# One written plan for five rounds of a mixed DFT and attention loop: the products with v in six blocks instead of ten, and the six score banks dealt in turn

## The chip, the cores and the metric

The kernel runs on one core of a Trainium2 chip. The metric is device time in microseconds (us): 1810.5 us is the median of three runs of the kernel before (1808.91 to 1810.7).

A core has engines that run their own queues of instructions in order: TensorE (PE in the profile, with its weight loads on a row of their own, PEld), VectorE (DVE), ScalarE (ACT), GpSimd (POOL) and SyncE (SP), which here issues nearly all transfers. PE writes its results into PSUM, which this kernel uses as eight banks of 128 x 512 float32; DVE and ACT read them from there.

## The reference, cut to what matters

```python
a = x @ dft_hid_re.T ; b = x @ dft_hid_im.T          # x: 2048 x 640
y = dft_seq_re @ a - dft_seq_im @ b                  # 2048 x 2048 matrices
q = (x @ wq) as 32 heads of 20 ; k = x @ wk ; v = x @ wv     # one k and v for all heads
p = softmax(q @ k.T * 20 ** -0.5)                    # per head 2048 x 2048
o = (p @ v) over heads @ wo
g = sigmoid((x * gate_w).sum(-1))
out = g * y + (1 - g) * o
```

Everything is float32. The kernel keeps that accuracy by splitting an operand into a high and a low part and adding three products.

## The kernel before, in words

**Before the main loop.** The first 250 us compute q, k, v and the gate, and then `a` and `b` of the hidden DFT (line 125), which go to DRAM and come back later as operands x. The first scores of the attention are computed there already.

**The main loop** mixes three streams of matmuls on PE, from about 249 us to 1623 us of the span.

- *Scores.* The heads come in 16 pairs p. Head 0 of a pair lies in rows 0 to 63 of the array, head 1 in rows 64 to 127, so a score matmul uses one half of the array's rows. Each score is computed twice. In the first pass (`a_unit`, line 330) 128 queries against 512 keys go to a PSUM bank, and DVE takes their maximum (line 337). In the second pass (`b_unit`, line 750) 128 keys against 512 queries go to a bank, with the maximum already subtracted through two more rows of the operand `qs`, and ACT takes the exponential into one of 16 SBUF buffers `pt` (line 759). A bank can be written again when its reader has ended.
- *Sequence DFT* (`y`, line 645). It is done as seven products of half-size blocks, 56 groups in all. In the main loop a group is one output block of 128 x 320. Its sum of 96 matmuls is halved over the two halves of the array's rows, 48 for each (16 steps j of three matmuls). [...] `Halves.run` makes the first y of a half after a turn wait for a score's reader that comes after the other half's last y (`mark`). The operands of a group come in two parts of eight steps, which POOL splits into high and low parts (`split_c`, lines 450 to 455) in one of three rotating buffers `ch`, `cl`. The 25th y of a half is the first that needs the second part.
- *Products with v* (`av_step`, line 763), "V" for short. One V takes four `pt` tiles (one step kc of 128 keys for both heads and two blocks of queries) and uses all 128 rows of the array in four groups of 32 columns. It adds into the bank "V".

A matmul on one half of the rows runs beside one on the other half. PE issues in order, so the written order decides what runs beside what.

**The order** is written out by hand. A round has eight a, eight b, 18 or 20 y and two V. `ROUND_10` is used three times and `ROUND_9` twice in five rounds. In a word like `a1S2` the digit is the half of the rows and the rest is the bank: the six banks S0 to S5 are written out by name for every score. `c` is a `b` that takes the newest free `pt` buffer. `E0` empties F0 with ACT (line 671) once in five rounds, after which POOL adds the block to earlier ones where the product needs that (lines 693 and 698). Each round is: seven scores of half 1 and nearly all y of half 0, one b across, V, then the mirror image, V. Each V handles a step whose scores came in the round before. One group y takes five rounds, and there are 48 times five rounds before the last pair of heads, which has its own round (`ROUND_LAST`, 16 times, with the two V side by side).

**The chain between pairs.** The a of a pair run 12 units (of 64 per half) ahead of the b. When the last a of a pair has been read, `tick()` (called at every second a) counts on; three ticks later `a_final` is issued: DVE transposes the maxima (`mt`, line 351), POOL splits them (`ms`, lines 352 and 353), SP writes them to DRAM (`m_d`) and reads them back into rows 60, 61, 124 and 125 of `qs` (four transfers `qs<-m_d`). The first b of that pair needs them.

Of the kernel before, what the change touches and what calls it, by code (L numbers as in the profile page):

```python
# [18 lines left out]
S = 2048  # L19
# [4 lines left out]
NT = S // P  # L24
NPAIR = H // 2
LAST = NPAIR - 1
HALF = D // 2
SJ = NT // 2
# [6 lines left out]
def kernel(  # L35
# [18 lines left out]
    psum = ctx.enter_context(tc.tile_pool(name="psum", bufs=1, space=PSUM))  # L54


    BANKS = {"A": ["S2", "S3", "S4"], "B": ["S0", "S1"], "F": ["S5", "F0"]}
    turn = {k: 0 for k in BANKS}

    def bank(tag, name):  # L60
# [308 lines left out]
    def tick():  # L369
        clock["n"] += 1  # L370
        due = [t for t in todo if t[0] <= clock["n"]]
        todo[:] = [t for t in todo if t[0] > clock["n"]]
        for _, f, args in due:
            f(*args)
# [4 lines left out]
    def a_half(hh, tag="A", main=False):  # L379
        u = state[hh]  # L380
        if u >= NA:
            return
        ins = a_unit(u, hh, tag)
        if main:
            halves.scored(ins)
        state[hh] = u + 1
        if state[1 - hh] <= u:
            return
        if u % 64 == 16 and u // 64 + 1 < NPAIR:
            load_qs(u // 64 + 1)  # L390
        if u % 64 == 63:
            later(1, a_reduce, u // 64)
            later(3, a_final, u // 64)
# [233 lines left out]
    class Halves:  # L627
# [3 lines left out]
            self.todo = [[], []]  # L631
            self.last = self.mark = None

        def put(self, ps2, w, x, start, stop):

            one = len(ps2) == 1
            for g, r in enumerate(RG):
                s0, s1 = start and not (one and g == 1), stop and not (one and g == 0)
                self.todo[g].append((ps2, w[r], x[r], s0, s1))

        def run(self, g):
            while not self.todo[g]:
                next(ys)
            ps, w, x, start, stop = self.todo[g].pop(0)
            mm = nc.tensor.matmul(ps[g % len(ps)], w, x, start=start, stop=stop)  # L645
            if len(ps) == 1:

                if not start and self.last != g:
                    tc.add_manual_dep(mm.ins, self.mark.ins.name, ORDER, reason="turns with a bank")
                self.last, self.mark = g, None  # L650
# [6 lines left out]
    halves = Halves()  # L657
# [3 lines left out]
    def y_evict():  # L661

        if not ended:
            return
        grp = ended[0]
        ps = grp["ps"]
        if "t" not in grp:
            grp["t"] = [op.tile([P, HALF], F32, name=("yt", "yu")[k]) for k in range(len(ps))]
            grp["left"] = list(range(len(ps)))
        k = grp["left"].pop(0)  # L670
        nc.scalar.activation(grp["t"][k], ps[k], AF.Copy)  # L671
        if not grp["left"]:
            ended.pop(0)
            y_out(grp)
# [4 lines left out]
    def y_in(n, k):  # L679

        got = []
        for q, (_, old, _) in enumerate(PRODUCTS[n][2]):
            if old is not None:
                t = op.tile([P, HALF], F32, tag=f"ya{q}", name="ya")
                move(t, y_block(old, k))
                got.append(t)
        return got
# [15 lines left out]
    def f_stream():  # L703

        load_c(0, 1)
        split_c(0, 1)  # L710
        for g, (n, k) in enumerate(GROUPS):
            ps = [bank("F0", f"y_{n}_{k}")[:, :HALF]]
            if g >= GMAIN:
                ps.append(bank("S5", f"y_{n}_{k}_1")[:, :HALF])
            y0 = y_in(n, k)
            for sh in range(2):
                h, l = c_ops.pop((g, sh))
                load_c(g + 1, sh)
                for j in range(SJ):
                    if j == SJ // 2:  # L720
                        split_c(g + 1, sh)
                        if sh == 0:
                            load_x(n + 1, k)
                        else:
                            split_x(n + 1, k)
                    jj = sh * SJ + j
                    x = x_ops[n, jj // 2]
                    hi, lo = x[:, jj % 2], x[:, 2 + jj % 2]
                    last = jj == NT - 1
                    halves.put(ps, h[:, j], hi, jj == 0, False)  # L730
                    halves.put(ps, h[:, j], lo, False, False)
                    halves.put(ps, l[:, j], hi, False, last)
                    if last:
                        ended.append({"n": n, "k": k, "ps": ps, "y": y0})
                    yield

# [7 lines left out]

    ptfree = list(range(16))

    def b_unit(p, hh, kc, qc, tag, newest):
        b = 64 * hh
        ps = bank(tag, f"b_{p}_{kc}_{qc}_{hh}")
        nc.tensor.matmul(  # L750
            ps,
            ks[b : b + 62, kc * P : (kc + 1) * P],
            qs[p][b : b + 62, qc * ROW : (qc + 1) * ROW],
            start=True,
            stop=True,
        )
        slot = ptfree.pop(-1 if newest else 0)
        t = pp.tile([P, ROW], F32, tag=f"pt{slot}", name="pt")
        halves.scored(nc.scalar.activation(t, ps, AF.Exp, scale=SCALE))  # L759
        pt[(hh, kc, qc)] = t, slot  # L760
# [4 lines left out]
    def av_step(p, qh, kc):  # L765
        if kc == 0:
            av[qh] = bank("V", f"av_{p}_{qh}")
        for hh in range(2):
            for j in range(2):
                t, slot = pt.pop((hh, kc, 2 * qh + j))  # L770
                av_mm(av[qh], 2 * hh + j, t, kc, kc == 0, kc == NT - 1)
                ptfree.append(slot)

    def finish_half(p, qh):
        ob = op.tile([P, ROW], F32, name="ob")
        nc.scalar.activation(ob, av[qh], AF.Copy)
        for hh in range(2):
            h = 2 * p + hh
            for j in range(2):
                js = slice((2 * qh + j) * ROW, (2 * qh + j + 1) * ROW)  # L780
                g = 32 * (2 * hh + j)
                move(sum_d[h : h + 1, js], ob[g + DH : g + DH + 1])
                move(oT_d[h * DH : (h + 1) * DH, js], ob[g : g + DH])
        if p == LAST:
            sm = op.tile([P, 16], F32, name="sm")
            ts = slice(qh * S // 2, (qh + 1) * S // 2)
            for hh in range(2):
                move(sm[64 * hh : 64 * hh + 64], sum_d[2 * p + hh, ts].rearrange("(s t) -> s t", t=16))
            later(4, finish_last, ts, sm)
        elif qh == 1:  # L790
            sm = op.tile([P, 32], F32, name="sm")
            move(sm, sum_d[2 * p : 2 * p + 2].rearrange("h (s t) -> (h s) t", t=32))
            later(24, finish_sums, p, sm)
# [11 lines left out]
    def finish_last(ts, sm):  # L805
# [10 lines left out]

    ROUND_10 = (
        "a1S0 y0 b1S3 y0 y0 c1S1 y0 y0 a1S2 y0 a1S5 y0 y0 a1S4 y0 b1S0 c0S3 V a0S1 y1 y1 b0S0 "  # L820
        "y1 y1 a0S5 y1 a0S3 y1 y1 b0S2 y1 y1 a0S4 y1 c0S0 c1S1 V y0"
    ).split()
    ROUND_9 = (
        "a1S2 y0 b1S0 y0 y0 a1S1 y0 a1S5 y0 y0 a1S4 y0 y0 b1S3 y0 c0S2 c1S0 V a0S5 y1 b0S2 y1 "
        "y1 a0S1 y1 c0S0 y1 y1 a0S3 y1 y1 a0S4 y1 E0 b1S2 c0S5 V"
    ).split()

    ROUND_LAST = (
# [3 lines left out]
    ).split()  # L832
    ROUNDS = [(p, qh, kk) for p in range(NPAIR) for qh in range(2) for kk in range(NT // 2)]

    BEFORE = {
        4: (lambda: load_wo(range(3)), lambda: load_o(0), lambda: load_o(1)),
# [1 line left out]
        6: (lambda: split_o(0), lambda: load_o(2)),  # L838
        7: (lambda: [load_y(tb) for tb in range(4)],),
    }  # L840
    old = []
    for rnd in ROUNDS:
        p, qh, kk = rnd
        nb, na = [0, 0], 0
        turn = (p * NT + qh * SJ + kk) % 5
        new = [(p, qh, 2 * kk), (p, qh, 2 * kk + 1)]
        for what in ROUND_LAST if p == LAST else ROUND_10 if turn < 3 else ROUND_9:
            if what == "V":
                if old:
                    st = old.pop(0)  # L850
                    av_step(*st)
                    if st[2] == NT - 1:
                        finish_half(*st[:2])
                continue
            g = int(what[1])
            if what[0] == "y":
                halves.run(g)
            elif what[0] == "E":
                if p == LAST or turn == 4:
                    y_evict()  # L860
            elif what[0] in "bc":
                b_unit(p, g, 2 * kk + nb[g] // 2, 2 * qh + nb[g] % 2, what[2:], what[0] == "c")
                if p == LAST and sum(nb) % 2 == 0:
                    tick()
                nb[g] += 1
            else:
                if na % 2 == 0:
                    tick()
                a_half(g, what[2:], True)
                na += 1  # L870
        old += new
        if p == LAST and qh == 1:
            for f in BEFORE.get(kk, ()):
                f()
    for _ in range(2):
        y_evict()
    split_o(1)
# [69 lines left out]
```

## Time and profile before

| What | Value |
|---|---|
| median of three runs | 1810.5 us |
| profiled execution: its span | 1807.7 us |
| rest, median less span | 2.8 us |
| PE busy | 1799.4 us (100%) |
| DVE busy | 1457.3 us (81%) |
| ACT busy | 1243.2 us (69%) |
| POOL busy | 822.1 us (45%) |
| granted PE clock, mean | 1.000 |

The columns of a group are: line, engine, operation, what it writes and reads, count, then busy time in us and mean ns of one, then idle time of the engine before them and what ended it. In a timeline the columns are start in us, length in us, engine, line, operation and count; neighbours of the same kind are merged into one row, "x8" says how many. One V shows as "x8", because each of its four matmuls stands twice in the records. Lengths of matmuls include their way through the array, so they overlap; the distance between starts is what one costs.

### The profile page before, as it was taken

Reading aid. Unit: us, or ns where it says so; the run is one execution under the profiler, and the core shown is the slowest. Engines: PE = TensorE matmul, PEld = TensorE weight load, DVE = VectorE, ACT = ScalarE, POOL = GpSimd, SP = SyncE. Lnnn points to the kernel's source line nnn. Section 1 sums busy time; section 2 is a strip of 40 time slices with the busy share of each in tenths; the row PEclk is TensorE's granted clock in tenths of the full one; section 3 lists DMA queues with packets and bytes.
Section 4 is the critical chain, followed back from the end, with each engine's and each line's share of the span. In section 5 each row is a group of like instructions: output and inputs, shape, how many; then the busy total and the mean of one; then the engine's idle time right before and its main releaser. Section 6 shows DMA issues by size and latency. Waiting matters only on the chain.

```text
span 1807.7 us, 40911 instructions
## 1 busy us (share of the span) xinstructions
PE 1799.4 (100%) x16342; PEld 1215.1 (67%) x16342; DVE 1457.3 (81%) x2335; ACT 1243.2 (69%) x2327; POOL 822.1 (45%) x559
## 2 busy tenths in 40 slices
PE   9999999999999999999999999999999999999999
PEld 7799976666666666666666666666666666657789
DVE  4469988888888888888888888888888888853354
ACT  5432247777777777777777777777777777776731
POOL 1012136444546464666655565565554444342241
PEclk9999999999999999999999999999999999999999
DMA  8763334332344433444353434353433342315666
GB/s 267 227 192 99 115 100 139 116 108 84 130 125 133 121 119 106 153 126 152 112 167 101 156 112 141 113 153 115 136 112 114 87 126 79 97 59 169 207 215 209
DMA packets 131003, 243.89 MB, mean 135 GB/s; under 512 B 26356, under 2 KB 77556, under 8 KB 128292
## 3 DMA queue, kind: packets, MB, share of 16 engines
q1 hardware_dynamic: 130012, 238.00, 41.8%
q0 software_dynamic: 800, 3.28, 0.6%
q8 instruction: 128, 2.10, 0.5%
q14 instruction: 63, 0.52, 0.1%
HBM read 194.62 MB, written 50.86 MB: 136 GB/s over the span
## 4 chain that ended last, share of the span: by engine, by line
PE 99%; DMA 0%; POOL 0%; ACT 0%; DVE 0%; issue 0%; SPq 0%; ACTq 0%
PE av L763 28%; PE y L645 20%; PE a L330 18%; PE b L750 15%; PE ab L125 8%; PE q L114 1%; PE o L114 1%; PE q L115 1%; PE q L116 1%; PE o L116 1%; PE o L115 1%; PE kv L210 0%; PE kv L211 0%; DMA xr<-in_xT_dram 0%; DMA xr<-x_d 0%; ACT pt L759 0%
## 5 line engine op out<-in xcount | busy, mean ns | idle before, releaser
L337 DVE TENSOR_REDUCE mx<-a 128x1 f32<-128x512 f32 x2048 | 1291.3, 684 | 170.0 <-PE a L330 164.6
L759 ACT ACTIVATE pt<-b 128x512 f32<-128x512 f32 x2048 | 1110.7, 597 | 334.9 <-PE b L750 289.9
L645 PE MATMUL y<-x,ch 64*128 64x320 f32 x3584 | 796.6, 317 | 1.1 <-ACT pt L759 1.1
L330 PE MATMUL a<-ks,qs 60*128 60x512 f32 x2048 | 740.0, 416 | 0.0
L645 PEld LDWEIGHTS y<-x,ch 64*128 64x128 f32 x3584 | 552.3, 184 | 85.5 <-ACT pt L759 83.5
L750 PE MATMUL b<-qs,ks 62*128 62x512 f32 x2048 | 596.5, 405 | 0.6 <-DVE mx L337 0.6
L330 PEld LDWEIGHTS a<-ks,qs 60*128 60x128 f32 x2048 | 379.8, 185 | 277.0 <-ACT pt L759 197.4
L763 PE MATMUL av<-pt,vsb 128*32 128x512 f32 x4096 | 542.0, 604 | 0.0
L645 PE MATMUL y<-x,cl 64*128 64x320 f32 x1792 | 528.3, 311 | 0.5 <-POOL cl L455 0.5
L645 PEld LDWEIGHTS y<-x,cl 64*128 64x128 f32 x1792 | 314.7, 184 | 42.0 <-ACT pt L759 41.1
L750 PEld LDWEIGHTS b<-qs,ks 62*128 62x128 f32 x2048 | 314.0, 185 | 23.4 <-issue 6.7
L450 POOL TENSOR_TENSOR craw<-craw 128x1024 f32<-128x1024 f32 x80 | 191.1, 2388 | 236.2 <-DMA craw<-in_cre_dram 88.8
L455 POOL TENSOR_TENSOR cl<-craw,ch 128x1024 fp32r<-128x1024 f32 x98 | 234.2, 2389 | 7.9
L454 POOL CAST ch<-craw 128x1024 fp32r<-128x1024 f32 x98 | 101.7, 1038 | 182.2 <-PE y L645 153.4
L763 PEld LDWEIGHTS av<-pt,vsb 128*32 128x32 f32 x4096 | 82.3, 108 | 139.8 <-issue 131.5
L125 PE MATMUL ab<-wh,xh 64*128 64x320 f32 x640 | 136.0, 307 | 0.0
L125 PE MATMUL ab<-wl,xh 64*128 64x320 f32 x640 | 135.8, 306 | 0.0
L125 PE MATMUL ab<-wh,xl 64*128 64x320 f32 x640 | 135.6, 305 | 0.0
L698 POOL TENSOR_TENSOR ya<-yt,ya 128x320 f32<-128x320 f32 x64 | 59.4, 944 | 142.8 <-ACT yt L671 142.2
L524 ACT ACTIVATE half<-ab 128x320 f32<-128x320 f32 x64 | 28.0, 438 | 114.1 <-PE ab L125 100.8
L125 PEld LDWEIGHTS ab<-wh,xl 64*128 64x128 f32 x640 | 98.7, 184 | 0.0
L125 PEld LDWEIGHTS ab<-wl,xh 64*128 64x128 f32 x640 | 98.6, 185 | 0.0
(88 smaller groups left out, 1082.7 us busy)
## 6 DMA issues: line engine op xcount, KB each, us to landing
craw<-in_cre_dram SPq DMA_DIRECT2D x96, 512.0 KB
craw<-in_cim_dram SPq DMA_DIRECT2D x96, 512.0 KB
xr<-x_d SPq DMA_DIRECT2D x88, 320.0 KB
qs<-qh_d SPq DMA_DIRECT2D x64, 160.0 KB
x_d<-both SPq DMA_DIRECT2D x64, 160.0 KB
ya<-y_d SPq DMA_DIRECT2D x64, 160.0 KB
y_d<-ya SPq DMA_DIRECT2D x64, 160.0 KB
xr<-in_xT_dram SPq DMA_DIRECT2D x20, 256.0 KB
```

Source lines behind the costliest of these rows:

```text
L114: nc.tensor.matmul(ps, wh, xh, start=(i == 0), stop=False)
L125: nc.tensor.matmul(ps, w[r], x[r], start=(i == 0 and k == 0), stop=(i == n - 1 and k == 2))
L330: nc.tensor.matmul(ps, qs[p][b : b + 60, qb * P : (qb + 1) * P], ks[b : b + 60, c * ROW : (c + 1) * ROW], start=True, stop=True,)
L337: return nc.vector.tensor_reduce(mx[p][:, hh, qb, c : c + 1], ps, axis=AX.X, op=ALU.max)
L450: eng.tensor_tensor(raw, raw, raws[1], op=PRODUCTS[n][0][1])
L454: eng.tensor_copy(h, raw)
L455: eng.tensor_tensor(l, raw, h.bitcast(F32), op=ALU.subtract)
L645: mm = nc.tensor.matmul(ps[g % len(ps)], w, x, start=start, stop=stop)
L698: nc.gpsimd.tensor_tensor(ya, yt, ya, op=how)
L750: nc.tensor.matmul(ps, ks[b : b + 62, kc * P : (kc + 1) * P], qs[p][b : b + 62, qc * ROW : (qc + 1) * ROW], start=True, stop=True,)
L759: halves.scored(nc.scalar.activation(t, ps, AF.Exp, scale=SCALE))
L763: nc.tensor.matmul(ps[32 * g : 32 * g + 32, :], vsb[:, kc, :], t, start=first, stop=last)
```

## The change

The rounds of five are replaced by one string `PLAN`, one letter for each instruction, which runs 48 times. Lower case is half 0 of the rows, capitals half 1: a/A and b/B are scores, y/Y the DFT, V a product with v, E the emptying of F0.

- The counts in a plan are those of five rounds before: 40 a, 40 b, 48 y and 48 Y, ten V and one E.
- The ten V stand in six blocks: two alone and four pairs. Between them lie stretches of 7, 46, 6, 18, 65 and 35 matmuls (the first reaches over the seam of two plans).
- The y of a plan are no longer mixed in ten turns of nine or ten: first 27 Y, then 9 y and 39 y, then 21 Y.
- The scores take the banks S0 to S5 in turn, whatever their reader, instead of by name.
- Every b takes the newest free `pt` buffer.
- A V handles the step that is two V behind (`LAG`); the scores are counted for each half by itself.
- `start` and `stop` of a group are decided when a matmul is issued, since either half may come first.
- `ROUND_LAST` and what follows are the same, written with the new counters.

```diff
-    BANKS = {"A": ["S2", "S3", "S4"], "B": ["S0", "S1"], "F": ["S5", "F0"]}
+    BANKS = {"S": ["S0", "S1", "S2", "S3", "S4", "S5"], "A": ["S2", "S3", "S4"], "B": ["S0", "S1"], "F": ["S5", "F0"]}
...
-            ps, w, x, start, stop = self.todo[g].pop(0)
+            ps, w, x, grp = self.todo[g].pop(0)
+            one = len(ps) == 1
+            k = 0 if one else g
+            start, stop = grp[k] == 0, grp[k] == (6 if one else 3) * NT - 1
+            grp[k] += 1
...
-        slot = ptfree.pop(-1 if newest else 0)
+        slot = ptfree.pop(-1)
...
-    ROUND_10 = (
-        "a1S0 y0 b1S3 y0 y0 c1S1 y0 y0 a1S2 y0 a1S5 y0 y0 a1S4 y0 b1S0 c0S3 V a0S1 y1 y1 b0S0 "
-        "y1 y1 a0S5 y1 a0S3 y1 y1 b0S2 y1 y1 a0S4 y1 c0S0 c1S1 V y0"
-    ).split()
-    ROUND_9 = (
-        "a1S2 y0 b1S0 y0 y0 a1S1 y0 a1S5 y0 y0 a1S4 y0 y0 b1S3 y0 c0S2 c1S0 V a0S5 y1 b0S2 y1 "
-        "y1 a0S1 y1 c0S0 y1 y1 a0S3 y1 y1 a0S4 y1 E0 b1S2 c0S5 V"
-    ).split()
+    PLAN = (
+        "BVaBYaYYbYYbYYaYbYYaYYbYaYYbYbYYaYbYYYaYbYYYaYaBVAbAaBbVVBayByyyAyByAyaAyByV"
+        "VAbyByAyyByyAyyByyAyByyAyyByyAyByByyyAyByAyyByByyAyAyyyAyByAyybAVVAbYYaYbY"
+        "YbYaYYbYaYYYaYYbYaYYbYaYYbYVVaBbAaE"
+    )
...
+    LAG = 2
+    taken = {"b": [0, 0], "a": 0, "V": 0}
+
+    def next_b(g, tag):
+        r, nb = divmod(taken["b"][g], 4)
+        p, qh, kc = STEPS[2 * r + nb // 2]
+        b_unit(p, g, kc, 2 * qh + nb % 2, tag)
+        taken["b"][g] += 1
+
+    def next_v():
+        st = taken["V"] - LAG
+        taken["V"] += 1
+        if st >= 0:
+            av_step(*STEPS[st])
+            if STEPS[st][2] == NT - 1:
+                finish_half(*STEPS[st][:2])
+
+    for what in PLAN * (LAST * NT // 5):
+        g = int(what in "ABY")
+        if what == "V":
+            next_v()
+        elif what == "E":
+            y_evict()
+        elif what in "yY":
+            halves.run(g)
+        elif what in "bB":
+            next_b(g, "S")
+        else:
+            if taken["a"] % 2 == 0:
+                tick()
+            a_half(g, "S", True)
+            taken["a"] += 1
```

More of the change, by code (lines that the diff above doesn't have):

```diff
@@ L632, in __init__, with put @@
             self.last = self.mark = None
-        def put(self, ps2, w, x, start, stop):
-            one = len(ps2) == 1
+        def put(self, ps2, w, x, grp):
             for g, r in enumerate(RG):
-                s0, s1 = start and not (one and g == 1), stop and not (one and g == 0)
-                self.todo[g].append((ps2, w[r], x[r], s0, s1))
+                self.todo[g].append((ps2, w[r], x[r], grp))
         def run(self, g):
@@ L643, in run @@
                 next(ys)
-            ps, w, x, start, stop = self.todo[g].pop(0)
+            ps, w, x, grp = self.todo[g].pop(0)
[3 more added lines that the diff above has]
+            grp[k] += 1
             mm = nc.tensor.matmul(ps[g % len(ps)], w, x, start=start, stop=stop)
-            if len(ps) == 1:
+            if one:
                 if not start and self.last != g:
@@ L715, in f_stream @@
             y0 = y_in(n, k)
+            grp = [0, 0]
             for sh in range(2):
@@ L728, in f_stream @@
                     hi, lo = x[:, jj % 2], x[:, 2 + jj % 2]
[L729 to L733, printed above, removed]
+                    halves.put(ps, h[:, j], hi, grp)
+                    halves.put(ps, h[:, j], lo, grp)
+                    halves.put(ps, l[:, j], hi, grp)
+                    if jj == NT - 1:
                         ended.append({"n": n, "k": k, "ps": ps, "y": y0})
@@ L745, with b_unit @@
     ptfree = list(range(16))
-    def b_unit(p, hh, kc, qc, tag, newest):
+    def b_unit(p, hh, kc, qc, tag):
         b = 64 * hh
@@ L812, in finish_last @@
             move(rx_d[h * DH : (h + 1) * DH, ts], rec_d[h : h + 1, ts].to_broadcast([DH, S // 2]))
-    ROUND_10 = (
-        "a1S0 y0 b1S3 y0 y0 c1S1 y0 y0 a1S2 y0 a1S5 y0 y0 a1S4 y0 b1S0 c0S3 V a0S1 y1 y1 b0S0 "
-        "y1 y1 a0S5 y1 a0S3 y1 y1 b0S2 y1 y1 a0S4 y1 c0S0 c1S1 V y0"
-    ).split()
-    ROUND_9 = (
-        "a1S2 y0 b1S0 y0 y0 a1S1 y0 a1S5 y0 y0 a1S4 y0 y0 b1S3 y0 c0S2 c1S0 V a0S5 y1 b0S2 y1 "
-        "y1 a0S1 y1 c0S0 y1 y1 a0S3 y1 y1 a0S4 y1 E0 b1S2 c0S5 V"
-    ).split()
+    PLAN = (
+        "BVaBYaYYbYYbYYaYbYYaYYbYaYYbYbYYaYbYYYaYbYYYaYaBVAbAaBbVVBayByyyAyByAyaAyByV"
+        "VAbyByAyyByyAyyByyAyByyAyyByyAyByyByyyAyByyAyyByByyAyAyyyAyByAyybAVVAbYYaYbY"
+        "YbYaYYbYaYYYaYYbYaYYbYaYYbYVVaBbAaE"
+    )
     ROUND_LAST = (
@@ L832 @@
     ).split()
-    ROUNDS = [(p, qh, kk) for p in range(NPAIR) for qh in range(2) for kk in range(NT // 2)]
+    STEPS = [(p, qh, kc) for p in range(NPAIR) for qh in range(2) for kc in range(NT)]
     BEFORE = {
@@ L840 @@
     }
[L841 to L847, printed above, removed]
-            if what == "V":
[L849 to L857, printed above, removed]
-            elif what[0] == "E":
[L859 to L863, printed above, removed]
-                    tick()
[L865 to L874, printed above, removed]
@@ L875 @@
+    for kk in range(NT):
+        for what in ROUND_LAST:
+            if what == "V":
+                next_v()
+            elif what[0] == "E":
+                y_evict()
+            elif what[0] == "y":
+                halves.run(int(what[1]))
+            else:
+                if sum(taken["b"]) % 2 == 0:
+                    tick()
+                next_b(int(what[1]), what[2:])
+        for f in BEFORE.get(kk - NT // 2, ()):
+            f()
+    old = STEPS[-LAG:]
     for _ in range(2):
```

## The prediction

> **What bounds the kernel now.** I read the page first, then the main loop alone (262 to 1620 us) as one stretch with PE's own list of waits, then the chain and PE's timeline.
>
> ```profile
> span 1807.7 us, 40911 instructions
> PE 1799.4 (100%) x16342; PEld 1215.1 (67%) x16342; DVE 1457.3 (81%) x2335; ACT 1243.2 (69%) x2327; POOL 822.1 (45%) x559
> L337 DVE TENSOR_REDUCE mx<-a 128x1 f32<-128x512 f32 x2048 | 1291.3, 684 | 170.0 <-PE a L330 164.6
> L759 ACT ACTIVATE pt<-b 128x512 f32<-128x512 f32 x2048 | 1110.7, 597 | 334.9 <-PE b L750 289.9
> ```
> ```profile
> 262.00:1620.00 1358.00, 1358.00 (x12107) 826.60 (x12107) 1187.97 (x1922) 1056.21 (x1970) 729.36 (x482) 1.00 0.39 120
> ```
> ```profile
> PE y L645 <- POOL cl L455: 0.5, 1, 0.5
> ```
>
> PE never stands still between 262 and 1620 us at full clock (1.00), and its one wait there is 0.5 us. DVE and ACT do stand still, and they wait for PE. So PE's written order is the time, and five rounds take, by two rows of the chain 36 cycles apart, (1312.48 - 279.89)/36 = 28.68 us:
>
> ```profile
> 279.89 1.01 PE av L763 x8
> ...
> 1312.48 1.02 PE av L763 x8
> ```
>
> **What one thing costs on PE.** A stretch between two V, from PE's timeline, and a pair of V from the last rounds:
>
> ```profile
> 1158.67 0.50 PE L330 MATMUL a<-ks,qs 60*128 60x512 f32 x1
> 1158.67 0.56 PE L645 MATMUL y<-x,ch 64*128 64x320 f32 x2
> 1159.01 0.40 PE L750 MATMUL b<-qs,ks 62*128 62x512 f32 x1
> 1159.07 0.31 PE L645 MATMUL y<-x,cl 64*128 64x320 f32 x1
> ...
> 1159.95 0.39 PE L330 MATMUL a<-ks,qs 60*128 60x512 f32 x1
> 1159.95 0.31 PE L645 MATMUL y<-x,cl 64*128 64x320 f32 x1
> ...
> 1160.52 1.06 PE L763 MATMUL av<-pt,vsb 128*32 128x512 f32 x8
> 1161.52 0.49 PE L330 MATMUL a<-ks,qs 60*128 60x512 f32 x1
> ```
> ```profile
> 1650.32 1.92 PE L763 MATMUL av<-pt,vsb 128*32 128x512 f32 x16
> 1652.17 0.73 PE L750 MATMUL b<-qs,ks 62*128 62x512 f32 x3
> ```
>
> Between 1159.0 and 1159.95 lie four scores (0.235 us each) and six y (0.147 each), side by side. The first score of a stretch takes 1159.01 - 1158.67 = 0.34, so a start costs 0.105. V to next start is 1.00 alone (0.995 before rounding) and 1652.17 - 1650.32 = 1.855 for two: 0.135 less than two alone. A stretch's floor is its fuller half: in six of the ten, 10 y and a score = 1.70; in four, seven scores = 1.64; together 16.8. With ten V, 16.8 + 9.95 = 26.75; the missing 1.93 are starts and ends, 0.195 for each stretch.
>
> **The change, part by part.**
>
> *PE's order.* The fuller half of the new stretches: 7 matmuls 3 scores = 0.70; 46: 27 Y and 2 B = 4.43; 6: 0.70; 18: 9 y and 2 a = 1.79; 65: 39 y and 2 b = 6.19; 35: 21 Y and A = 3.31. Sum 17.13, which is 0.36 more, since y pile up on one half. V: 2 x 0.995 + 4 x 1.855 = 9.41, 0.54 less. Starts and ends: 6 x 0.195 = 1.17, 0.78 less. Sum 27.71, so -0.96 us a cycle. All of it is on the path, as PE is.
>
> *Six banks in turn.* Now the n-th score waits for the reader of the (n-6)th, and a stretch holds up to 13 a. The readers' pace, and the delay from a score's start to its reader's:
>
> ```profile
> 602.28 0.20 DVE L351 STREAM_TRANSPOSE mt<-mxr 128x32 f32<-128x32 f32 x1
> 602.65 2.48 DVE L337 TENSOR_REDUCE mx<-a 128x1 f32<-128x512 f32 x4 [0.17 <-PE a L330]
> ```
> ```profile
> 602.12 0.50 PE L330 MATMUL a<-ks,qs 60*128 60x512 f32 x1
> ```
> ```profile
> 612.50 1.57 ACT L759 ACTIVATE pt<-b 128x512 f32<-128x512 f32 x3 [0.35 <-PE y L645]
> ```
>
> DVE: (2.48 - 0.68)/3 = 0.60 each, 0.53 after the score's start. ACT: (1.57 - 0.60)/2 = 0.49. Over a cycle that is 40 x 0.60 = 24.0 and 40 x 0.49 = 19.6, both under 27.7. Inside the stretches it is tight. In the 46, the last B needs the bank of the sixth a: 0.53 + 5 x 0.60 + 0.68 = 4.2, plus 0.05 for the release (below) 4.3; PE is there at 0.105 + 0.235 + 27 x 0.147 = 4.3. In the 65, the last A needs the ninth A: 0.53 + 8 x 0.60 + 0.68 + 0.05 = 6.1; PE is there at 6.1. In the 35 it is 3.1 against 3.2. The pairs of V need an exponential whose score stands last or last but one ahead of them: 0.53 + 0.60 after that score, while PE has a first V of 0.88 in between. So no stretch has a margin over 0.1. Bounds: 0 (all fits), and 0.13 for each of six stretches, 0.8. I take 0.25, near the low end, because every sum above comes out within 0.1 of PE. Cycle: -0.71.
>
> *The first cycle.* The second part of the first group is split late:
>
> ```profile
> 255.87 2.37 POOL L450 TENSOR_TENSOR craw<-craw 128x1024 f32<-128x1024 f32 x1 [10.82 <-DMA xr<-x_d]
> 258.30 1.04 POOL L454 CAST ch<-craw 128x1024 fp32r<-128x1024 f32 x1
> 259.42 2.37 POOL L455 TENSOR_TENSOR cl<-craw,ch 128x1024 fp32r<-128x1024 f32 x1
> ```
> ```profile
> 249.30 0.49 PE L750 MATMUL b<-qs,ks 62*128 62x512 f32 x1 [0.62 <-DVE mx L337]
> ...
> 261.84 0.41 PE L645 MATMUL y<-x,cl 64*128 64x320 f32 x1 [0.52 <-POOL cl L455]
> ...
> 278.00 0.49 PE L330 MATMUL a<-ks,qs 60*128 60x512 f32 x1
> ```
>
> Before, the 27th y of a half met this at its place in round 3 and waited 0.52 (cl ends at 261.79, so the release takes 0.05). Now 27 Y stand at the front: Y27 is reached at 249.3 + 4.2 = 253.5 and waits until 261.84, 8.3 us, with everything behind it. The first cycle is 27.71 less two V that have nothing to do yet (2 x 1.19) plus 8.3 = 33.6, where before it ended at 278.00, 28.7. So +4.9, once. Later groups are split a cycle ahead: POOL has 45% to do, and the order puts their 25th Y 14 us behind the release of their buffer.
>
> *The chain between pairs.* The a lead by 12 units. In rounds, that was always three rounds; in the plan it depends on where a pair's seam falls, and there are five places, (64p) mod 20, each met three times.
>
> ```profile
> 602.55 0.21 POOL L352 CAST ms<-mt 128x32 fp32r<-128x32 f32 x1 [6.76 <-DVE mt L351]
> ```
> ```profile
> 603.12 0.32 SPq L106 DMA_DIRECT2D m_d<-ms  x1
> 605.46 0.33 SPq L106 DMA_DIRECT2D craw<-in_cim_dram  x1
> 605.89 2.50 SPq L106 DMA_DIRECT2D qs<-m_d  x4
> ```
> ```profile
> 878.46 0.32 SPq L106 DMA_DIRECT2D m_d<-ms  x1
> 879.95 2.51 SPq L106 DMA_DIRECT2D qs<-m_d  x4
> ```
> ```profile
> 616.85 0.39 PE L750 MATMUL b<-qs,ks 62*128 62x512 f32 x1
> ```
>
> Before: mt at 602.28, the pair's first b at 616.85, 14.6 us later. The chain needs 602.28 to 605.89 = 3.6 to the first `qs<-m_d` when a load of craw stands between on SP's queue (it waits for POOL's next sum), else 0.84 + 1.49 = 2.3; the four take 2.5; the last lands, by the 1.49 in which `m_d` was written and seen, 1.49 after its issue. So half 1 has its rows 3.6 + 2.5 - 0.6 + 1.5 = 7.0 after mt (5.7 without the load), half 0 1.25 earlier.
>
> - p = 4, 9, 14: the last A of the pair stands in the 18, mt comes after the third A of the 65 (0.53 + 3 x 0.60 = 2.3 into it), and the pair's first B is the ninth B there, behind 24 y (0.105 + 0.235 + 24 x 0.147 = 3.9). Rows at 2.3 + 7.0 = 9.3: PE waits 5.4, and again 5.4; for p = 14 no load stands between, 4.1. Sum 14.9. Behind that B wait both halves and all V; DVE and ACT run dry.
> - p = 2, 7, 12: mt after the 7 (2.3), first b in the 6, at 0.70 + 0.195 + 0.995 + 4.63 + 0.995 = 7.5. Rows of half 0 at 2.3 + 5.7 = 8.0. For 7 and 12 POOL first has two and one sums of y of 0.94 us. I take 0.4, 1.9 and 0.7: 3.0.
> - The other three places have 9 us or more between mt and the first b (the next one is mt 4.7 into the 65 and the first B of the next plan 13.8 into it): nothing.
>
> Together +17.9. Bounds: 0, if the rows land much sooner, and 25, if all six wait for 7.0 and a POOL operation of 2.4 us.
>
> [...]
>
> *The rest.* Turns of y go from ten to two, and each has a V or more as cover, as before: nothing. Newest-first buffers: a b's exponential comes behind its V on PE anyway: nothing. If that cover were missing, a wait of at most one exponential, 0.6. SP issues the same transfers.
>
> **Sum.** 47 x (-0.71) + 4.9 + 17.9 = -10.6 on a span of 1807.7, so 1797.1; with 2.8 around it 1799.9, and 1810.5 - 10.6 = 1799.9 for the median.
>
> **Rivals.**
>
> *The seams cost nothing:* the rows land before B needs them, say because SP and POOL run ahead. For it: before, no b ever waited for `qs`. Against it: a distance of 3.9 - 2.3 = 1.6 us, where the two transfers alone need 2 x 1.49. Then -33.4 + 4.9 = -28.5: 1782.
>
> *The banks bind (slower).* For it: sums without margin, and a bank dealt in turn hands an ACT delay on to a, and a DVE delay on to b. At 0.8 a cycle: 47 x (-0.16) + 22.8 = +15.3: 1826. From 0.96 - 22.8/47 = 0.47 a cycle on the kernel gets slower. Against it: the readers have 3.7 us a cycle to spare and four pairs of V of 1.855 in which to catch up.
> [...]
>
> *A pair of V does not save:* its second step waits for its exponential in three of four pairs, 0.2 each: -0.11 a cycle: 47 x (-0.11) + 22.8 = +17.6: 1828. For it: those scores stand last. Against: the 0.88 of the first V.
>
> **Chances.** Forecast 0.50 (1790 to 1809); seams free 0.17; banks 0.25; pairs 0.08. 0.2%, 3.6 us, is about what tells a measurement here from no change. Of the forecast's 0.50, 0.40 lies under 1806.9, 0.07 within 0.2% and 0.03 above; of the banks' 0.25, 0.02 within. Faster: 0.17 + 0.40 = 0.57; same: 0.07 + 0.02 = 0.09; slower: 0.03 + 0.23 + 0.08 = 0.34. The range is from just below the free seams to the last rival, 1778 to 1828.
>
> **What would show it.** Right: from one V to the same V a cycle later 27.9 to 28.0; four rows "av x16" a cycle; one wait of y for `cl` of about 8 us near 253; three waits of b for `qs<-m_d` of 4 to 6 us, near cycles 12, 28 and 44; DVE's idle time less. Wrong: waits of a and b for `mx` and `pt` over 0.5 a cycle (the banks), waits of av for `pt` (the pairs), or no wait for `qs`.

## The result, and the profile after

The changed kernel takes 1832.1 us (median of four runs, 1831.08 to 1833.34), the kernel before 1809.7 us in the same comparison (1808.91 to 1810.7). The ratio is 1.0125, 95% interval 1.0111 to 1.0139: the change makes the kernel 1.25% slower. The prediction of 1799.9 us was wrong, and the time lies above its range of 1778 to 1828 us.

From the page of the changed kernel, the span, the engines' busy times and the groups of the two kinds of reader; lines past 635 now stand two further down (V is line 765, y 647, b 752, exponentials 761):

```profile
span 1831.3 us, 41016 instructions
PE 1792.0 (98%) x16342; PEld 1278.5 (70%) x16342; DVE 1426.2 (78%) x2335; ACT 1187.1 (65%) x2327; POOL 823.5 (45%) x559
L337 DVE TENSOR_REDUCE mx<-a 128x1 f32<-128x512 f32 x2048 | 1262.8, 681 | 229.0 <-PE a L330 127.3
L761 ACT ACTIVATE pt<-b 128x512 f32<-128x512 f32 x2048 | 1058.7, 619 | 385.2 <-PE b L752 227.7
```

PE was busy 100% of the span and is busy 98%. It stands still now, and its own list of waits says for what (total, times, longest):

```profile
PE b L752 <- DMA qs<-m_d: 23.7, 6, 5.7
PE y L647 <- POOL ch L454: 6.2, 1, 6.2
PE y L647 <- POOL cl L455: 1.5, 1, 1.5
```

Six waits of the first b of a pair for its rows of `qs`, 23.7 us, and one stand of 7.7 us, in two parts, for the operands of the first group of y. DVE's idle time before the maxima went up (170.0 to 229.0), where the prediction had named less of it as a sign of being right. The clean part of the loop, from the chain (start, length, what):

```profile
1001.59 1.85 PE av L765 x16
1006.96 1.85 PE av L765 x16
1009.70 1.00 PE av L765 x8
1015.40 0.99 PE av L765 x8
1017.29 1.85 PE av L765 x16
1021.23 1.92 PE av L765 x16
...
1029.76 1.85 PE av L765 x16
```

Four pairs and two single V to a cycle of 1029.76 - 1001.59 = 28.17 us; it was 28.68. So the plan does shorten a cycle, but not to the forecast 27.9 to 28.0 us. Against the span of before (+23.6 us), from the distances between one stretch of 65 and the next (28.25 is the mean, with some cycles of 28.4 to 28.5 us in it):

| Part | forecast | measured |
|---|---|---|
| 47 cycles, without what seams add | 47 x (-0.71) = -33.4 | 47 x (28.25 - 28.68) = -20.2 |
| first cycle | +4.9 | 37.0 - 28.7 = +8.3 |
| seams between pairs, six cycles | +17.9 | +34.7 |
| rest | 0 | +0.8 |
| sum | -10.6 | +23.6 |

**One seam.** Timelines of DVE, POOL, SP and PE around the start of pair 4 (start, length, engine, line, operation; in brackets the idle time ahead and its cause):

```profile
616.66 0.20 DVE L351 STREAM_TRANSPOSE mt<-mxr 128x32 f32<-128x32 f32 x1
```
```profile
617.43 2.37 POOL L450 TENSOR_TENSOR craw<-craw 128x1024 f32<-128x1024 f32 x1
```
```profile
617.50 0.33 SPq L106 DMA_DIRECT2D m_d<-ms  x1
619.83 0.33 SPq L106 DMA_DIRECT2D craw<-in_cim_dram  x1
620.26 2.50 SPq L106 DMA_DIRECT2D qs<-m_d  x4
```
```profile
614.33 0.49 PE L330 MATMUL a<-ks,qs 60*128 60x512 f32 x1
...
618.64 0.30 PE L647 MATMUL y<-x,ch 64*128 64x320 f32 x1
624.40 0.76 PE L752 MATMUL b<-qs,ks 62*128 62x512 f32 x1 [5.46 <-DMA qs<-m_d]
```

The chain is the one that the prediction wrote down: maxima, split, write, a load of craw on SP's queue that waits for POOL's sum, four reads, b. The four issues are 2.50/4 = 0.63 apart, so the last starts at 622.17, and b follows 2.23 us later.

**What comes after a wait.** Stretches of 3.4 us around the seam of pair 2 (columns: time, busy us of PE, its weight loads, DVE, ACT and POOL, then PE's granted clock, then the transfers):

```profile
434.00:437.40 3.40, 1.94 (x14) 0.85 (x14) 1.91 (x5) 0.77 (x3) 1.78 (x1) 1.00 0.55 143
437.40:440.80 3.40, 3.40 (x18) 0.88 (x12) 0.68 (x2) 0.99 (x3) 1.20 (x1) 0.50 0.35 131
440.80:444.20 3.40, 3.40 (x34) 2.04 (x32) 3.02 (x5) 2.17 (x4) 1.18 (x1) 1.00 0.00 0
```
```profile
437.12 3.42 PE L765 MATMUL av<-pt,vsb 128*32 128x512 f32 x16
440.47 0.64 PE L752 MATMUL b<-qs,ks 62*128 62x512 f32 x1
```

In the first row PE stands still for 1.46 us of the 3.4. In the second it works without a gap, at half clock: the pair of V that starts at 437.12 takes 3.35 us to the next start, where a pair in the clean loop takes 1.85. The clock's records show such windows, 3.41 or 6.83 us long, at all six seams. The time in them in which PE works is lost by half: 1.7, 2.1, 1.7, 1.6, 1.7 and 2.0 us, together 10.8. With the 23.7 us of waits that is 34.5 of the 34.7 us of the seams. The shortest of the six waits, 1.46 us, was enough for it.

The first cycle has the same in small: PE's stand until 260.17 and again until 262.60, and a clock of 0.5 from 256.49 to 266.73.

### The profile page after: what moved, and what is told of

It reads as the page before. It is cut to its first block, busy times and chain, and to the rows that moved or that the text cites. A ratio compares the mean times of both kernels' runs of the same rounds, so it can differ in the third digit from the quotient of the medians.

```text
span 1831.3 us, 41016 instructions
## 1 busy us (share of the span) xinstructions
PE 1792.0 (98%) x16342; PEld 1278.5 (70%) x16342; DVE 1426.2 (78%) x2335; ACT 1187.1 (65%) x2327; POOL 823.5 (45%) x559
## 4 chain that ended last, share of the span: by engine, by line
PE 96%; DMA 2%; POOL 1%; SPq 1%; issue 0%; ACT 0%; DVE 0%; POOLq 0%; DVEq 0%
PE av L765 26%; PE y L647 20%; PE a L330 18%; PE b L752 15%; PE ab L125 8%; PE q L114 1%; PE o L114 1%; PE q L115 1%; PE q L116 1%; PE o L116 1%; PE o L115 1%; DMA qs<-m_d 1%; POOL craw L450 1%; SPq L106 1%; DMA m_d<-ms 0%; PE kv L210 0%
## 5 line engine op out<-in xcount | busy, mean ns | idle before, releaser
L337 DVE TENSOR_REDUCE mx<-a 128x1 f32<-128x512 f32 x2048 | 1262.8, 681 | 229.0 <-PE a L330 127.3
L761 ACT ACTIVATE pt<-b 128x512 f32<-128x512 f32 x2048 | 1058.7, 619 | 385.2 <-PE b L752 227.7
L752 PE MATMUL b<-qs,ks 62*128 62x512 f32 x2048 | 789.0, 438 | 23.7 <-DMA qs<-m_d 23.7
L647 PE MATMUL y<-x,ch 64*128 64x320 f32 x3584 | 758.7, 309 | 7.5 <-POOL ch L454 6.2
L647 PEld LDWEIGHTS y<-x,ch 64*128 64x128 f32 x3584 | 571.7, 185 | 13.9 <-POOL ch L454 6.5
L765 PE MATMUL av<-pt,vsb 128*32 128x512 f32 x4096 | 507.3, 605 | 0.0
L330 PEld LDWEIGHTS a<-ks,qs 60*128 60x128 f32 x2048 | 356.1, 186 | 202.1 <-DVE mx L337 157.6
L752 PEld LDWEIGHTS b<-qs,ks 62*128 62x128 f32 x2048 | 351.4, 186 | 109.6 <-DVE mx L337 40.8
L765 PEld LDWEIGHTS av<-pt,vsb 128*32 128x32 f32 x4096 | 112.7, 109 | 199.9 <-issue 160.8
```

The costliest lines, as they stand in the source:

```text
L330: nc.tensor.matmul(ps, qs[p][b : b + 60, qb * P : (qb + 1) * P], ks[b : b + 60, c * ROW : (c + 1) * ROW], start=True, stop=True,)
L337: return nc.vector.tensor_reduce(mx[p][:, hh, qb, c : c + 1], ps, axis=AX.X, op=ALU.max)
L752: nc.tensor.matmul(ps, ks[b : b + 62, kc * P : (kc + 1) * P], qs[p][b : b + 62, qc * ROW : (qc + 1) * ROW], start=True, stop=True,)
L765: nc.tensor.matmul(ps[32 * g : 32 * g + 32, :], vsb[:, kc, :], t, start=first, stop=last)
```

## Experiments

**The seams, and the first cycle.** The first theory was that the slower time is the waits at the seams with their half clock, and the stand in the first cycle; the rival, that the banks in turn hold PE back everywhere.

```diff
-    LEAD = 12
+    LEAD = 16
```

> The changed kernel with the a 16 units ahead of the b where there were 12; nothing else differs. Theory (the seams between pairs): the six waits of b for qs<-m_d (23.7 us) and the half clock that follows each of them go together, so the six cycles that take 31.7 to 35.7 us fall to about 28.3, 34.7 us less in all, less about 1 us for eight more scores ahead of the loop: 1798 us (1795 to 1801), granted clock 1.00 from 270 us to the end of the loop. Rival (the clock falls for a reason of its own, such as the denser stretches): only the 23.7 us of waits go, 1808 us, and half-clock windows stay inside the loop. Rival (the seams are not the loss, the banks are): under 5 us change, 1827 or more.

Measured: 1800.7 us, ratio to the kernel before 0.9947 (0.993 to 0.9963). That is 31.4 us less than the changed kernel, by one number: the units by which the a run ahead of the b. Four units more put eight more scores ahead of the loop, and the maxima of a pair are read back four ticks earlier. No wait for `qs` is left in the main loop, and no half clock after the first cycle (mean granted clock 0.997, where the changed kernel has 0.988), so the half clock came from the waits. The other two waits stay:

```profile
PE y L647 <- POOL ch L454: 6.1, 1, 6.1
PE y L647 <- POOL cl L455: 1.5, 1, 1.5
```

So the seams made the change a loss. The same number in the kernel before:

> The kernel before with reads four ticks earlier (LEAD 16). Theory: the old order has no wait for the transposed reads, so nothing is to be had there: 1810 us, 1808 to 1812. Rival: an earlier read helps the old order too (what LEAD 16 brought is no matter of the new order): 1800 us or less.

Measured: 1810.8 us, 1.0007 (0.9998 to 1.0016). The old order had nothing to gain from earlier reads, so what LEAD 16 brings is a matter of the new order.

The first cycle alone: the first of the 48 plans in the order of the old five rounds (`ROUNDS`, the words of before written as letters, banks still in turn).

```diff
-    for what in PLAN * (LAST * NT // 5):
+    for what in ROUNDS + PLAN * (LAST * NT // 5 - 1):
```

> The changed kernel with the first of its 48 plans in the order of the five rounds before (banks in turn there too); nothing else differs. Theory (27 y at the front meet the late split of the first group): the two waits of y for ch and cl (6.2 and 1.5 us) go, with the half clock after them, and the first cycle falls from 37.0 to about 29 us: 1824 us (1822 to 1826). Rival (POOL is late anyway and the wait moves into the second cycle): 1830 or more.

Measured: 1828.5 us, 1.0101 (1.0086 to 1.0116), 3.7 us less than the changed kernel where 8 were expected. The first cycle did go from 37.0 to 29.4 us, but the main loop starts 1.3 us later, by its first b, and the six seam cycles sum to 1.3 us more. Both edits together:

> Both edits at once: the a 16 units ahead, and the first plan in the order of the rounds before. Theory: the two losses lie at different places and add up, 34.7 - 1 + 8 = 42 us less than the changed kernel: 1790 us (1787 to 1793), 1% under the kernel before. What is left of the change is then 28.2 us a cycle against 28.68. Rival (the losses overlap, or a longer lead brings a new wait, such as qs being loaded into a buffer that b still reads): 1797 or more.

Measured: 1791.5 us, 0.9897 (0.9883 to 0.9912), clock 1.000. With the two waits gone, the plan is 1% faster than the kernel before.

**How short a wait costs the clock.** `LEAD` 14 and 15 in the changed kernel leave shorter waits at the seams.

> The changed kernel with reads two ticks earlier (LEAD 14 where it is 12). With LEAD 12 the six waits for the transposed reads are 1.46, 5.46, 3.64, 5.45, 2.01 and 5.72 us; a tick is about 1.41 us (28.2 us by 20 ticks), so two ticks leave 2.6, 0.8, 2.6 and 2.9 us, 9 us in four waits, none of 3.4 us. Without any of these waits (LEAD 16) the kernel took 1800.7 us. Theory: every wait of TensorE of about a microsecond or more is followed by a window at half clock that ends some 3.4 us on and costs about 1.9 us, so 1800.7 + 9 + 4 x 0.3 for restarts + 4 x 1.9 = 1818.5 us, 1815 to 1821. Rival: waits this short leave the clock alone: 1800.7 + 9 + 1.2 = 1811 us, 1809 to 1813.

Measured: 1815.2 us, 1.0032 (1.0019 to 1.0045), between both expectations. The waits are 2.09, 2.33, 2.07, 1.48 and 1.69 us, with a sixth of 0.22, but only three of them are followed by half clock (620.85, 1078.24 and 1535.62 us, each 3.41 us long). Two waits of this run, one with and one without:

```profile
617.40:620.80 3.40, 1.31 (x15) 1.08 (x14) 1.12 (x3) 1.33 (x4) 3.34 (x3) 1.00 0.46 131
620.80:624.30 3.50, 3.50 (x24) 1.70 (x24) 3.00 (x5) 1.74 (x4) 2.26 (x2) 0.51 0.92 169
```
```profile
1351.30:1354.70 3.40, 1.92 (x14) 0.80 (x16) 1.88 (x4) 1.07 (x3) 1.06 (x1) 1.00 0.49 154
1354.70:1358.00 3.30, 3.30 (x34) 1.94 (x31) 1.85 (x4) 2.08 (x5) 2.25 (x1) 1.00 0.10 38
```

The half-clock windows begin at whole multiples of 3.413 us from one another: from 620.85 to 1078.24 it is 134 times that, and in the changed kernel from 437.40 to 621.72 it is 54 times, with records 3.413, 6.827 and 10.240 us long. On that grid the three waits with half clock lie within one window (1.69 to 2.09 us of its 3.41), while the wait of 2.33 us lies across an edge, 0.79 us before it and 1.55 after. So neither theory was right: not every wait of a microsecond costs the clock, and waits well under the 3.41 us of a window can. PE's idle share of one window fits all but the smallest cases: 1.48 and 1.55 us in a window left the clock alone here, the 1.46 us of pair 2 above did not. What else counts there stays open. In the main loops of the changed kernel and of this one, half clock followed every window at full clock in which PE stood still for 1.69 us or more; of the three windows with 1.46, 1.48 and 1.55 us, only the first, that of pair 2 above, was followed by it.

> The changed kernel with reads three ticks earlier (LEAD 15): waits of about 1.2, 1.2 and 1.5 us are left at three seams. Theory (half clock after every wait of about a microsecond): 1800.7 + 3.9 + 3 x 0.3 + 3 x 1.7 = 1810.6 us, 1807 to 1813. Rival (the clock stays): 1805.5 us, 1804 to 1807.

Measured: 1801.6 us, 0.9957 (0.994 to 0.9973). Waits of 0.96, 1.72 and 0.85 us (the profile puts the last down to a maximum on VectorE), and no half clock after any of them (the 1.72 is cut by an edge into 0.24 and 1.48). The rival is right on the clock and too high on the time: the cycles with those three waits are 1.1, 1.9 and 1.0 us longer than in the kernel with LEAD 16, but the first stretch of 65 starts 2.0 us earlier, and some other cycles are 0.1 to 0.2 shorter. So the theory that every short wait costs the clock falls.

**Banks in turn, or the choice of buffers.** The prediction had put the loss of a slower case on the banks, and nothing on the buffers. The old order of the five rounds in all 48 cycles, with the changed kernel's banks in turn and newest buffers:

```diff
-    for what in PLAN * (LAST * NT // 5):
+    for what in ROUNDS * (LAST * NT // 5):
```

> The order of the five rounds before, kept in all 48 cycles and written as letters; the six banks dealt in turn and the newest buffer for every b, as in the change. Theory (dealing costs only where a stretch holds more scores than the readers can take): eight scores in 1.9 us and a V after them fit, so a cycle stays at 28.68 us, no half clock, 1810 us (1808 to 1812). Rival (a bank dealt in turn hands waits from ACT to DVE and back wherever it is used): 0.45 us more a cycle as in the changed kernel, 1831 us.

Measured: 1826.1 us, 1.0089 (1.0073 to 1.0104), 16 us above the theory. The old order with banks in turn and newest buffers is slow without any wait in PE's list: its stretches of 18 and 17 matmuls take 1.91 us each (medians) where they took 1.89 and 1.85. To part banks from buffers, the same kernel with the old rule for buffers (the c of the old words marked again):

```diff
-        slot = ptfree.pop(-1)
+        slot = ptfree.pop(-1 if newest else 0)
```

> The old order of the five rounds in all 48 cycles, six score banks in turn, but the old rule for the exponentials' buffers (first in the row of free ones, last in the row for the four marked scores of a round). Theory: the old order with banks in turn is slow through the exponentials that must wait for an earlier exponential as well as for TensorE (the buffer's last writer is one that nothing has waited for yet); there are 160 of them in the kernel before, 827 in the old order with banks in turn and newest buffers (15.8 us longer), 494 here, so (494 - 160) / 667 x 15.8 = +7.9 us: 1818 us, 1815 to 1821. Rival: the turn of the banks itself costs it, and the buffers nothing: 1826 us, 1824 to 1828. Second rival: the count does not matter, only the rule for buffers: 1810 us.

Measured: 1809.6 us, 1.0003 (0.9993 to 1.0012), below the theory's range and as the second rival said. In the old order, banks in turn cost nothing. And the reverse, the kernel before with one edit:

```diff
-        slot = ptfree.pop(-1 if newest else 0)
+        slot = ptfree.pop(-1)
```

> The kernel before with one edit: every exponential takes the newest free buffer; order and named banks stay. 588 exponentials wait for an earlier one. Theory (the second wait costs): (588 - 160) / 667 x 15.8 = +10.1 us, 1820 us, 1816 to 1823. Rival (the banks' turn costs it, buffers nothing, as the prediction had it): 1810 us, 1808.5 to 1811.

Measured: 1828.0 us, 1.0108 (1.0093 to 1.0123). The buffers alone cost 19.2 us, above the range of the theory, with the banks as they were. The views of the exponentials' line in the kernel before, in this one and in the one with banks in turn and old buffers (operation, count, duration, first and last start):

```profile
L759 ACTq EVENT_SEMAPHORE  x160: 17/17/17, 268.6 to 1731.0; - x160
```
```profile
L759 ACTq EVENT_SEMAPHORE  x588: 17/17/17, 256.9 to 1742.5; - x196
```
```profile
L761 ACTq EVENT_SEMAPHORE  x494: 17/17/17, 259.9 to 1732.1; - x165
```

An exponential waits for its score on PE. If the last writer of its buffer is an exponential that ACT has not yet waited for, it waits for that too. Then one of the two waits becomes an instruction of its own, 17 ns long in these views, which stands in this count, and the exponential comes behind it. The counts of 494 and 588 were worked out by this rule ahead of the runs, and the traces have the same. Where ACT stands idle, that shows at the start. The kernel with newest buffers and the one with old buffers, each with a score that ends while ACT is idle:

```profile
1161.67 0.39 PE L750 MATMUL b<-qs,ks 62*128 62x512 f32 x1
```
```profile
1162.16 2.19 ACT L759 ACTIVATE pt<-b 128x512 f32<-128x512 f32 x4 [0.64 <-PE b L750]
```
```profile
1160.05 0.40 PE L752 MATMUL b<-qs,ks 62*128 62x512 f32 x1
```
```profile
1160.49 0.60 ACT L761 ACTIVATE pt<-b 128x512 f32<-128x512 f32 x1 [0.36 <-PE b L752]
```

The start comes 0.10 us after the score's end in the first, 0.04 in the second; over all such starts the medians are 0.097 and 0.037. The plain count of second waits is not what costs, as 494 of them cost nothing: none of those came on an idle ACT. Counted in the traces from 300 to 1580 us, second waits on an idle ACT number 0 in the kernel before, 0 with old buffers and banks in turn, 466 in the old order with banks in turn and newest buffers, 465 in the kernel before with newest buffers. The times above the kernel before are 0, 0.8, 15.8 and 19.2 us. A third choice of buffers has 254 second waits, most of them at bad places:

```diff
+        old = [s for s in ptfree if wrote[s] <= seen[1]]
+        slot = old[-1] if old else max(ptfree, key=lambda s: wrote[s])
+        ptfree.remove(slot)
+        seen[0] += 1
+        seen[1] = max(seen[1], wrote[slot])
+        wrote[slot] = seen[0]
-        slot = ptfree.pop(-1)
```

> The old order of the five rounds in all 48 cycles, six score banks in turn, and each exponential takes a free buffer whose last writer lies no later than the latest exponential that has been waited for; only where none is free, the one last written. 254 exponentials then wait for an earlier one. Theory (the second wait of an exponential is what costs): (254 - 160) / 667 x 15.8 = +2.2 us, 1812 us, 1809 to 1815. Rival (the turn of the banks costs it): 1826 us, 1824 to 1828.

Measured: 1819.0 us, 1.0059 (1.0042 to 1.0076): between the two. 198 of its second waits meet an idle ACT, and it is 10.1 us over the kernel before. So it is 0.03 to 0.05 us for each second wait on an idle ACT. The way from there to PE is argued: the last score of a stretch waits for a bank which an exponential gives back, so that an exponential that starts 0.06 us late ends the stretch that much later. The stretches of 17 fit it, 1.91 us for 1.85.

The same choice of buffers in the fastest kernel so far:

> The changed kernel with reads four ticks earlier (LEAD 16) and the first cycle in the old order, which took 1791.5 us, and buffers chosen so that only 113 exponentials wait for an earlier one, where that kernel had 308. Theory (the second wait costs, and the stretches of 18 and 65 that run .17 and .22 us over their sum are held by exponentials): (308 - 113) x 15.8 / 667 = 4.6 us less at most, 1787 to 1791 us, most likely 1789. Rival (the stretches wait for exponentials running back to back, which a later start within a gap does not change): 1791.5 us, 1790.5 to 1792.5.

Measured: 1786.6 us, 0.9879 (0.9864 to 0.9894), just below the theory's range and 4.9 us less than with newest buffers (3.4 by the distances of both to the kernel before on their own chip). Second waits on an idle ACT fall from 158 to 0, the stretch of 18 from 2.16 to 2.10 us and that of 65 from 6.61 to 6.55: 0.12 a cycle by the medians, 5.6 us in 47. The mean cycle falls by 0.09, from 28.28 to 28.18. This version beats both kernels, the one before by 22 us in the same comparison.

**Which reader holds the stretches.** They still stand over their sums (18: 2.10 against 1.79 + 0.195 = 1.985; 65: 6.55 against 6.385).

```diff
-        return nc.vector.tensor_reduce(mx[p][:, hh, qb, c : c + 1], ps, axis=AX.X, op=ALU.max)
+        return nc.vector.tensor_reduce(mx[p][:, hh, qb, c : c + 1], ps[:, : ROW // 2], axis=AX.X, op=ALU.max)
```

> The changed kernel with LEAD 16, the old order in the first cycle and buffers chosen for few second waits (1786.6 us), in which VectorE takes the maximum of each 128x512 score bank over 256 of its 512 columns alone: the other half of the columns is left out of the maximum. Its stretches of 18 and 65 matmuls run 2.10 and 6.55 us against sums of 1.985 and 6.385. Theory (their last scores wait for banks that back-to-back exponentials on ScalarE hold): the 65 stays above 6.5 and the 18 falls by at most its part that waits for VectorE, 0.05: 1784 to 1787 us. Rival (VectorE's maxima hold the banks): both fall to their sums, 0.28 x 46 = 12.9 us less, 1774 us, 1772 to 1777.

Measured: 1779.4 us, 0.9832 (0.9817 to 0.9846), between theory and rival. V from the chains, of the kernel with whole maxima and of the one with halved maxima; the 46 lies between two rows "x8", the 65 between the two rows "x16" that follow:

```profile
1010.99 1.00 PE av L772 x8
1016.68 0.99 PE av L772 x8
...
1022.58 1.92 PE av L772 x16
1031.04 1.86 PE av L772 x16
...
1039.17 1.00 PE av L772 x8
1045.17 1.00 PE av L772 x8
```
```profile
1008.49 1.00 PE av L772 x8
1014.11 1.00 PE av L772 x8
...
1020.02 1.92 PE av L772 x16
1028.48 1.85 PE av L772 x16
```

The 65 stays at 6.55 and the 18 at 2.10 (medians), as the theory says: there VectorE is not the limit. But the stretch of 46 falls from 4.70 to 4.62 us, its sum of 4.63, and the nine cycles of 45 that take 28.3 to 28.5 us go (in the last two rows of the first view such a 46 takes 5.0). In all nine, DVE also gathers and transposes the maxima of a pair (`mxr`, line 343, and `mt`, line 351); in three others it does so and they are not longer. The mean cycle falls from 28.18 to 28.02, so VectorE costs about 0.16 us a cycle, and what is left in the 18 and the 65 is not its doing. That it is ScalarE, whose exponentials start 0.478 us apart in the 65 of the changed kernel (1024.20 to 1028.50 us), fits the 0.12 that the choice of buffers took out of just these two stretches; no run shortened the exponentials themselves.

## Why the prediction was wrong

Two terms of the sum were too small. The seams were put at 17.9 us, with nothing for the clock, and cost 34.7; the banks were put at 0.25 us a cycle and what stands there is 0.54.

*Order, V pairs, starts and ends: right.* Four pairs and two single V, at 1.855 and 0.995 us as forecast, and the stretches without bank waits stand on their sums (35: 3.51 for 3.31 + 0.195). The stretch that is called 7 has six matmuls and the E; its three scores of one half are what was priced. The rival that pairs save nothing is out.

*Banks in turn: too small by half, and for another reason.* I took 0.25 us a cycle; the clean cycle of 28.16 is 0.45 over the floor of 27.71, and the mean without seams 28.25. The step that failed is "no stretch has a margin over 0.1 ... I take 0.25, near the low end". Of the 0.54, about 0.1 comes from second waits of the exponentials, and 0.16 from VectorE; that the rest, about 0.3, is ScalarE's pace is argued and not shown. Some scores inside a stretch have records of 0.49 in place of 0.39, and the next score of their half starts 0.1 later; that this is a restart after a short wait for a bank is not shown. The point of 0.47 from which the banks alone would have made the kernel slower was worked with seams of 17.9 us. With the measured seams and first cycle (43.0 us) the cycle would have had to be below 27.8 to come out even.

*"Newest-first buffers ... nothing": wrong.* The cover that I named, the V ahead on PE, has to do with when the buffer is free. What costs is the second wait on ACT's own queue, and the bank that is given back 0.06 us later. It is 3 to 6 us in the new order with LEAD 16, and 19.2 us in the old.

*The first cycle: right in its cause, too small.* The wait was forecast as 8.3 us and is 7.7; half clock until 266.73 stands behind it, which the step left out: about 5 us of work at half speed, 2.5 us. The remaining 1.5 us of the 3.4 stay open.

*The seams: the six places right, the price half of the truth.* The waits are 1.46, 3.64 and 2.01 us where I had 0.4, 1.9 and 0.7, and 5.46, 5.45 and 5.72 where I had 5.4, 5.4 and 4.1. Two transfers were priced by one row, 1.49. The last read is seen 2.23 us after its issue at pair 4 (in the six seams 2.2 to 2.9, by the issue that each b needs). At pair 14 no load stands between, as forecast, but from the write of `m_d` to the first read it took 3.0 us and not 1.49:

```profile
1545.89 0.32 SPq L106 DMA_DIRECT2D m_d<-ms  x1
1548.91 2.51 SPq L106 DMA_DIRECT2D qs<-m_d  x4
```

At pairs 4 and 9 the 5.4 came out right from two errors that cancel: the chain took 7.74 us for 7.0, and PE stood 2.28 us after `mt` for 1.6. The second is a miscount and not the banks. Ahead of the ninth B stand 28 y, where I counted 24: 0.105 + 0.235 + 28 x 0.147 = 4.46, and from the stretch's start at 614.33 that is 618.79, where the last y (618.64) has taken its 0.147. Then the clock, the larger part: 10.8 us of half speed behind the waits, which the step put at nothing. It had "Behind that B wait both halves and all V; DVE and ACT run dry" and went no further. By the granted clock of 1.00 in the loop before, the profile gave no hint of it, as PE never stood still there. Waits and clock are +16.8 us over the forecast, the cycles +13.2 and the first cycle +3.4: together 33.4, most of the distance from -10.6 to +23.6.

## What to carry to other kernels

A denser order of work moves every hand-over between streams: list each chain that runs over DRAM, work out its slack in the new order at each place where it can fall, and give it more lead before the order is judged; here four ticks turned a loss of 1.25% into a gain of 0.5%. Price a stand of TensorE at its length and the half clock behind it, here up to 2.1 us. Where a reader sits on a tight bank, choose its output buffers so that it needs no second wait: taking free buffers whose last writer had been waited for made the kernel with LEAD 16 and the old first cycle 4.9 us shorter (1791.5 to 1786.6; 3.4 by the distances to the kernel before).

## What the runs showed of the hardware that was not expected

- Half clock in windows of 3.41 us on a fixed grid, after waits as short as 1.46 us (changed kernel) and 1.69 to 2.09 us (LEAD 14) where they lie within one window; one of 1.48 us within a window (LEAD 14), and waits of 2.33 (LEAD 14) and 1.72 us (LEAD 15) that an edge cuts, left the clock at full speed.
- On an idle ACT an exponential with two waits started 0.06 us later than one with a single wait (0.097 against 0.037 us after the score's end); behind a running exponential the second wait cost nothing that could be measured (494 of them, the kernel 0.8 us over the one before).
- With no load between, the first read of `m_d` (32 KB in DRAM) was issued 1.45 to 1.49 us after the write at some pairs of the kernel before (7, 12, 14 and 15), 2.8 to 2.9 us after it at others (6 and 11), and 2.9 to 3.4 us after it in the changed kernel (6, 8, 11, 13 and 14). What makes the difference stays open.
